# Attention ahead of two MoE layers: row sums' epsilon on ScalarE, separate tiles for maxima, a later start for GpSimd

## The chip, the cores and the metric

The kernel runs on one core of one Trainium2 chip. The metric is the device time of one execution in microseconds; less is better. Engines are named as the profile names them: PE (TensorE matmuls), PEld (TensorE weight loads), DVE (VectorE), ACT (ScalarE), POOL (GpSimd), SP (SyncE, which issues the DMAs).

## The reference

Block-causal attention with 4 batches, 8 heads, 576 positions and a head dimension of 64, then two MoE-like layers on the 2304 tokens of 512 features. All is float32.

```python
scores = scale * np.matmul(q, k.transpose(0, 1, 3, 2))
scores = np.where(block_i >= block_j, scores, -1000000000.0)   # blocks of 64
scores = scores - np.max(scores, axis=-1, keepdims=True)
attn = np.exp(scores)
attn = attn / (np.sum(attn, axis=-1, keepdims=True) + 1e-09)
out = np.matmul(attn, v)
...
h = x @ w_in;  x = (h * np.clip(h + 3.0, 0.0, 6.0) / 6.0) @ w_out
h = x @ w_in2; x = (h * np.tanh(np.log1p(np.exp(h)))) @ w_out2
```

## The kernel before, in words

**Numbers as two parts.** Matmul operands are split into a high part and a remainder in the matmul's type (`hi = copy(x)`, `lo = x - hi`); a product is three matmuls, hi x hi, hi x lo and lo x hi. So each operand costs a copy on ACT or POOL and a subtraction on DVE or POOL.

**Attention.** Two heads that share 128 partitions are a pair; there are 16 pairs (`NP`), and five rounds to each, so 80 rounds g (`NG`). A round handles one or two query blocks of 64 (`PARTS`, in the order `TIME`): a big part and, in four of five rounds, a small one; together 320 or 640 columns of scores.

- `scores(g)` (L431) makes the scores in one of two PSUM tiles `s` (L442 to L444, three matmuls each). Then for each part DVE takes the negated maximum into a column of `nm` (L454), and ACT takes the exp with this maximum as bias, writes `p` and leaves the row sum in a column of `su` (L463). An exp is followed by an instruction that reads the accumulator.
- `transposes(g)` (L472) transposes `p` on PE (L495) into one of three PSUM banks `t`, from where ACT copies the high part to `z` (L281) and DVE subtracts the remainder (L287).
- `attn_v` (L505) multiplies with V into the PSUM tile `o` (L526), four calls for each pair; ACT copies `o` to `x` (L281), and DMAs store it.
- `sums(p)` (L539) takes the nine row sums of a pair (128 x 9), adds 1e-9 on DVE (L546), takes the reciprocal on DVE (L547), transposes on PE (L548) into a `t` bank, and ACT copies the result to `rs`.
- `split_q`, `split_k` and `split_v` prepare a pair's inputs. For pair 0 ACT and DVE split the queries (L372, L375) and ACT the high part of the keys (L397); the keys' remainder goes to DVE or POOL (L404). For later pairs all of it is POOL's work, and the split queries reach `qb` by two DMAs from `qs` (L388).
- `early_weights` (L559) prepares two of the first MoE layer's weight tiles in four pieces, in the rounds named by `EARLY_ROUNDS`.

**What sets the order.** The loop at L611 adds the operations of each round to a list: transposes of round g - `LAG_T` ahead of the scores when `FIRST_T` is true, behind them when it is not; the sums of a pair at a lag of `LAG_R` rounds; attention times V at a lag of `LAG_V`. `Schedule.order` (L129) then plans all engines with a table of costs (L64) and latencies. An operation's due time follows from the TensorE work listed ahead of what needs it; each engine takes, among the operations that are ready, the one due first. PE may choose among its next 40 (`AHEAD`) listed operations until the first MoE layer's second product begins, and goes by the list from there on. The planned order is then issued: each engine works through its own queue in this fixed order. The semaphores between engines are put in afterwards, from the tiles that the instructions read and write; one tile is one thing to wait for.

**MoE layers.** Behind attention the same list continues with the first MoE layer (`in1`, `out1`), whose weights are loaded and split while it runs, with the preparation of the second layer's weights beside it (`unit2`), and then the second layer (`in2`, `out2`). Their tiles take the memory of the attention tiles once these are closed (hooks `leave_scores` and `leave_attention`).

Of the kernel before, what the change touches and what calls it, by code (L numbers as in the profile page):

```python
# [9 lines left out]
F32 = mybir.dt.float32  # L10
F32R = mybir.dt.float32r
U32 = mybir.dt.uint32
AF = mybir.ActivationFunctionType
ALU = mybir.AluOpType
AX = mybir.AxisListType
# [3 lines left out]
P = 128  # L19
B, H, S, D = 4, 8, 576, 64  # L20
NB = S // 64
# [8 lines left out]
SCALE = 1.0 / math.sqrt(D)  # L30
# [15 lines left out]


LAND = 4500
EARLY_ROUNDS = (20, 32, 44, 56)
LAG_T, LAG_V, LAG_R, FIRST_T = 4, 10, 7, True  # L50

ALIGN = 96
NX = 384
# [161 lines left out]
def f32(ap):  # L215
    return ap.bitcast(F32)
# [7 lines left out]
def fused_kernel(ctx: ExitStack, tc: tile.TileContext, qT, kT, vv, w1, w2, outT):  # L224
    nc = tc.nc
# [13 lines left out]
    ident = cpool.tile([P, P], F32, tag="ident", name="ident")  # L239
# [25 lines left out]
    plan = Schedule()  # L265
# [19 lines left out]
    def sub(engines, reads, writes, dst, a, b, **kw):  # L285
        return plan.add(
            engines, reads, writes, lambda e: ENG[e].tensor_sub(*real(dst, a, b)), **kw)  # L287

    def matmuls(n, reads, writes, run):
        return plan.add((("PE", n, False),), reads, writes, run)  # L290
# [28 lines left out]
    for n in range(3):  # L319
        at["t", n] = ps_t.tile([P, 4, P], F32, tag="t", name=f"t{n}")  # L320
    for n in range(4):
        at["nm", n] = sm.tile([P, 2], F32, tag="nm", name=f"nm{n}")
    pairs = [(b, hp) for b in range(B) for hp in range(NPAIR)]
    NP = len(pairs)
    EARLY_TILES = (
# [34 lines left out]
    def warm():  # L360
        for n in range(20):
            nc.tensor.transpose(at["t", 0][:, n % 4, :], ident, ident)

    def split_q(p):
        n = p % 2
        q, qs = at["q", n], at["qs"]
        if p == 0:
            for j in range(2):
                r = slice(64 * j, 64 * j + 64)
                src = q[r].rearrange("p (n d) -> p n d", d=64)  # L370
                hi, lo = at["qb", 0][r, 0, :, r], at["qb", 0][r, 1, :, r]
                copy(S, [("q", n), ("qb", 0, j)], [("qb", 0, j, 0)], hi, src, scale=SCALE)  # L372
                plan.add(
                    one("DVE", "DVE", S), [("q", n), ("qb", 0, j, 0)], [("qb", 0, j)],
                    lambda e, lo=lo, src=src, hi=hi: nc.vector.scalar_tensor_tensor(  # L375
                        lo, src, SCALE, f32(hi), op0=ALU.mult, op1=ALU.subtract))
            return
        plan.add(
            one("POOL", "POOL_ONE", S), [("q", n)], [("q", n)],
            lambda e: nc.gpsimd.tensor_scalar(q, q, SCALE, 1.0, op0=ALU.mult, op1=ALU.mult))  # L380
        plan.add(
            one("POOL", "POOL_ONE", S), [("q", n)], [("qs", 0)], lambda e: nc.gpsimd.tensor_scalar(
                qs[:, 0, :], q, 1.0, 1.0, op0=ALU.mult, op1=ALU.mult))
        sub(one("POOL", "POOL", S), [("q", n), ("qs", 0)], [("qs", 1)], qs[:, 1, :], q,
            f32(qs[:, 0, :]))
        for j in range(2):
            r = slice(64 * j, 64 * j + 64)
            dma(288, [("qs", 0), ("qs", 1)], [("qb", n, j)], f32(at["qb", n][r, :, :, r]),  # L388
                f32(qs[r]).rearrange("p t (n d) -> p t n d", d=64), land=LAND)

    def split_k(p):
        n = p % 2
        k, kb = at["k", n], at["kb", n]

        def first(e):
            if e == "ACT":
                nc.scalar.activation(kb[:, 0, :], k, AF.Copy)  # L397
            else:
                nc.gpsimd.tensor_scalar(kb[:, 0, :], k, 1.0, 1.0, op0=ALU.mult, op1=ALU.mult)

        plan.add(
            one("ACT", "ACT", S) if p == 0 else one("POOL", "POOL_ONE", S), [("k", n)],
            [("kb", n, 0)], first)
        sub(either(S) if p == 0 else one("POOL", "POOL", S), [("k", n), ("kb", n, 0)],  # L404
            [("kb", n, 1)], kb[:, 1, :], k, f32(kb[:, 0, :]))

    def split_v(p):
        n = p % 2
        for i in range(2):
            r, c = ((slice(0, P), slice(0, 4)), (slice(0, 64), slice(4, 5)))[i]  # L410
            src = at["v", n][r, c, :].rearrange("p c (h d) -> p (c h) d", h=2)
            dst = at["vb", n][r, c].rearrange("p c h t d -> p (c h) t d")
            hi, lo = dst[:, :, 0, :], dst[:, :, 1, :]
            w = (512, 128)[i]
            plan.add(
                one("POOL", "POOL_V", w), [("v", n, i)], [("vb", n, i, 0)],
                lambda e, hi=hi, src=src: nc.gpsimd.tensor_scalar(
                    hi, src, 1.0, 1.0, op0=ALU.mult, op1=ALU.mult))
            sub(one("POOL", "POOL", w), [("v", n, i), ("vb", n, i, 0)], [("vb", n, i, 1)],
                lo, src, f32(hi))  # L420

# [9 lines left out]
    def scores(g):  # L431
# [5 lines left out]
        for i, _, o, banks in score_parts(m):  # L437
            n = 64 * (i + 1)
            for a, z, b in ((o, 512, 0), (512, o + n, 1)) if len(banks) == 2 else ((o, o + n, banks[0]),):
# [4 lines left out]
                    nc.tensor.matmul(sc[:, cs], ql[:, i, :], kb[:, 0, ks], start=False, stop=True)  # L444

                matmuls(3 * cost("S", z - a), names, [("s", g % 2)], run)
        nm, su = at["nm", g % 4], at["su", p % 2]
        t, w = parts[m]
        todo = score_parts(m)
        for i, c, o, banks in todo:  # L450
            n = 64 * (i + 1)
            plan.add(
                one("DVE", "DVE_PSUM", n), [("s", g % 2)], [("nm", g % 4, c)],
                lambda e, o=o, n=n, c=c: nc.vector.tensor_reduce(  # L454
                    nm[:, c:c + 1], sc[:, o:o + n], axis=AX.X, op=ALU.max, negate=True))
        for i, c, o, banks in todo:
            n = 64 * (i + 1)
            col = ORDER.index(i)
            dst = t[:, w:w + n] if c else t[:, 0:n]
            plan.add(  # L460
                one("ACT", "EXP", n), [("s", g % 2)] + [("nm", g % 4, c), ("pz", m, c)],
                [("p", m, c), ("su", p % 2, col)],
                lambda e, o=o, n=n, c=c, col=col, dst=dst: nc.scalar.activation(  # L463
                    dst, sc[:, o:o + n], AF.Exp, bias=nm[:, c:c + 1], accum_out=su[:, col:col + 1]))

    bank = [0]

# [71 lines left out]
    def sums(p):  # L539
        b, hp = pairs[p]  # L540
        su, rs, k = at["su", p % 2], at["rs", p % 2], next_bank()
        tp = at["t", k]
        cols = [("su", p % 2, i) for i in range(NB)]
        plan.add(
            one("DVE", "DVE", NB), cols, cols,
            lambda e: nc.vector.tensor_scalar(su, su, 1e-9, None, op0=ALU.add))  # L546
        plan.add(one("DVE", "DVE", NB), cols, cols, lambda e: nc.vector.reciprocal(su, su))  # L547
        matmuls(cost("T", P), cols, [("t", k)], lambda e: nc.tensor.transpose(tp[0:NB, 0, :], su, ident))  # L548
        copy(P, [("t", k)], [("rs", p % 2)], rs, tp[0:NB, 0, :], psum=True)
        dma(4, [("rs", p % 2)], [("rsd", hp, b)],  # L550
            rsd[hp, :, b * S:(b + 1) * S].rearrange("h (n q) -> n h q", q=64),
            rs.rearrange("n (h q) -> n h q", h=2))

    def prepare(p):
        if p < NP:
            split_k(p)
            split_q(p)

# [656 lines left out]
```

## Time and profile before

| | |
|---|---|
| median of 3 runs | 964.37 us (964.29 to 970.2) |
| profiled execution: its time / its span | 966.9 / 965.0 us |
| busy over the span | PE 940.8 (97%), PEld 855.0 (89%), DVE 619.7 (64%), ACT 535.1 (55%), POOL 610.4 (63%) |
| DMA | 212.88 MB, 221 GB/s in the mean |
| attention, about | 9 to 215 us |

The span runs from the first to the last instruction of the profiled execution; its time includes what lies around it. An engine's busy time counts its instructions, not its waits. In the view in order of time each row has the start and the length in us, the engine, the line, the operation, the tiles written and read, the shape, the number of instructions that were merged, and in brackets the idle time of the engine just before and what ended it. A row of POOL is rough in its length. Line 281 is the helper that makes every ACT copy and line 287 the one that makes the subtractions, so those rows are told apart by their tiles.

### The profile page before, as it was taken

To read this page: it belongs to the slowest core of one execution; us is meant where nothing else is said; L and a number is where in the kernel's file an instruction comes from. 1 tells how busy PE (TensorE), PEld (TensorE's weight loads), DVE (VectorE), ACT (ScalarE), POOL (GpSimd) and SP (SyncE) were. 2 spreads that over 40 slices of the span, in tenths; PEclk is the share of its full clock that TensorE was granted. 3 is DMA by queue.
4 is the path that set the end of the run, shared out by engine and by line. 5 is a ranking of instruction groups with operands and counts; after the bars stand their busy time and mean duration, and the time that the engine had idled before them with its cause. 6 is when DMAs were issued, how large, how long until landed. Compare 5 with 4: busy or idle time off the path is not lost.

```text
span 965.0 us, 15989 instructions
## 1 busy us (share of the span) xinstructions
PE 940.8 (97%) x5300; PEld 855.0 (89%) x5300; DVE 619.7 (64%) x1150; ACT 535.1 (55%) x1254; POOL 610.4 (63%) x640
## 2 busy tenths in 40 slices
PE   7989999999999999999999999999999999999998
PEld 6878888888888887877788899999999999999997
DVE  6778777778875566556422235566578756876567
ACT  5878888886765455454332243544464444644452
POOL 8577777636888556844500013386798876967875
PEclk9999999999999999999999999999999999999999
DMA  9597897459648898888610016776778876787752
GB/s 244 146 248 204 189 233 200 116 163 366 251 151 260 290 302 287 287 300 282 192 50 1 0 45 234 262 265 225 266 261 306 311 265 234 262 306 261 262 200 95
DMA packets 131426, 212.88 MB, mean 221 GB/s; under 512 B 45840, under 2 KB 72464, under 8 KB 131344
## 3 DMA queue, kind: packets, MB, share of 16 engines
q1 hardware_dynamic: 131344, 211.86, 68.1%
q8 instruction: 42, 0.69, 0.3%
q14 instruction: 40, 0.33, 0.1%
HBM read 154.66 MB, written 48.31 MB: 210 GB/s over the span
## 4 chain that ended last, share of the span: by engine, by line
PE 49%; DVE 1%; DMA 1%; ACT 0%; issue 0%; POOL 0%; DVEq 0%; POOLq 0%; SPq 0%
PE y L687 8%; PE y L688 8%; PE y L689 8%; PE h L687 5%; PE h L688 5%; PE h L689 5%; PE r L689 3%; PE r L688 3%; PE r L687 3%; DMA S<-x2d 1%; DVE o L1027 0%; POOL S L287 0%; DMA w2d<-S 0%; DVE e L287 0%; ACT X L281 0%
## 5 line engine op out<-in xcount | busy, mean ns | idle before, releaser
L687 PE MATMUL h<-X,wh 128*128 128x512 f32 (+1 forms) x320 | 119.6, 374 | 0.8 <-DVE gl L287 0.5
L688 PE MATMUL h<-X,wh 128*128 128x512 f32 (+1 forms) x320 | 118.0, 369 | 0.3 <-POOL X L287 0.3
L689 PE MATMUL h<-X,wl 128*128 128x512 f32 (+1 forms) x320 | 118.0, 369 | 0.0
L688 PE MATMUL y<-gl,wh 128*128 128x512 f32 (+1 forms) x320 | 117.7, 368 | 0.0
L687 PE MATMUL y<-gh,wh 128*128 128x512 f32 (+1 forms) x320 | 117.7, 368 | 0.0
L689 PE MATMUL y<-gh,wl 128*128 128x512 f32 (+1 forms) x320 | 117.7, 368 | 0.0
L687 PE MATMUL y<-X,wh 128*128 128x384 f32 x336 | 112.5, 335 | 1.1 <-ACT xs L281 0.9
L688 PE MATMUL y<-X,wh 128*128 128x384 f32 x336 | 112.5, 335 | 0.0
L689 PE MATMUL y<-X,wl 128*128 128x384 f32 x336 | 112.3, 334 | 0.0
L287 POOL TENSOR_TENSOR X<-xr,X 128x384 fp32r<-128x384 f32 (+2 forms) x35 | 38.0, 1088 | 110.9 <-ACT X L281 110.9
L793 DVE SCALAR_TENSOR_TENSOR h<-e,h 128x512 f32<-128x512 f32 (+1 forms) x64 | 40.1, 627 | 89.9 <-ACT e L281 89.8
L463 ACT ACTIVATE p<-s,nm 128x576 f32<-128x576 f32 (+2 forms) x144 | 76.0, 529 | 31.7 <-DVE nm L454 29.9
L1027 DVE TENSOR_TENSOR sgh<-y,sgh 128x384 f32<-128x384 f32 x129 | 69.6, 555 | 33.2 <-PE y L689 33.2
L287 DVE TENSOR_TENSOR z<-t,z 128x512 fp32r<-128x512 f32 (+3 forms) x144 | 73.0, 521 | 19.9 <-ACT z L281 18.5
L454 DVE TENSOR_REDUCE nm<-s 128x1 f32<-128x576 f32 (+2 forms) x144 | 67.1, 480 | 26.2 <-PE s L444 13.0
L281 ACT ACTIVATE e<-h 128x512 f32<-128x512 f32 (+1 forms) x80 | 43.9, 549 | 66.5 <-PE h L689 66.5
L287 POOL TENSOR_TENSOR X<-e,X 128x384 fp32r<-128x384 f32 x69 | 71.3, 1034 | 10.9 <-ACT X L281 10.9
L495 PE MATMUL t<-ident,p 128*128 128x128 f32 x400 | 66.6, 283 | 7.6 <-DVE z L287 6.6
L687 PEld LDWEIGHTS h<-X,wh 128*128 128x128 f32 x320 | 60.3, 189 | 14.3 <-DVE gl L287 4.8
L689 PEld LDWEIGHTS h<-X,wl 128*128 128x128 f32 x320 | 60.4, 189 | 10.4 <-DVE wl L740 0.2
L688 PEld LDWEIGHTS h<-X,wh 128*128 128x128 f32 x320 | 60.4, 189 | 10.2 <-POOL X L287 0.7
L689 PEld LDWEIGHTS y<-gh,wl 128*128 128x128 f32 x320 | 60.3, 188 | 10.0
(166 smaller groups left out, 2679.2 us busy)
## 6 DMA issues: line engine op xcount, KB each, us to landing
raw<-w SPq DMA_DIRECT2D x64, 512.0 KB
wh<-w2d SPq DMA_DIRECT2D x48, 512.0 KB
wl<-w2d SPq DMA_DIRECT2D x48, 512.0 KB
wh<-w2d SPq DMA_DIRECT2D x48, 384.0 KB
wl<-w2d SPq DMA_DIRECT2D x48, 384.0 KB
x1d<-x SPq DMA_DIRECT2D x64, 144.0 KB
qb<-qs SPq DMA_DIRECT2D x30, 288.0 KB
w2d<-Sh SPq DMA_DIRECT2D x32, 256.0 KB
```

The lines of the kernel that those rows point to most:

```text
L281: nc.scalar.activation(d, s, func, **kw)
L287: engines, reads, writes, lambda e: ENG[e].tensor_sub(*real(dst, a, b)), **kw)
L454: lambda e, o=o, n=n, c=c: nc.vector.tensor_reduce(nm[:, c:c + 1], sc[:, o:o + n], axis=AX.X, op=ALU.max, negate=True))
L463: lambda e, o=o, n=n, c=c, col=col, dst=dst: nc.scalar.activation(dst, sc[:, o:o + n], AF.Exp, bias=nm[:, c:c + 1], accum_out=su[:, col:co ...
L495: nc.tensor.transpose(tp[:, c, :], t[:, o:o + P], ident)
L687: nc.tensor.matmul(b, wh, xh, start=start and k == 0, stop=False, skip_group_check=True)
L688: nc.tensor.matmul(b, wh, xl, start=False, stop=False, skip_group_check=True)
L689: nc.tensor.matmul(b, wl, xh, start=False, stop=last, skip_group_check=True)
L793: nc.vector.scalar_tensor_tensor(g, e, 6.0, h, op0=ALU.min, op1=ALU.mult)
L1027: nc.vector.tensor_add(dst, src, old)
```

## The change

The maxima of the two parts of a round get a tile each, `nm0` and `nm1` (four buffers each), instead of two columns of one. In `sums`, ACT copies the nine sums with 1e-9 added into a `t` bank in PSUM, DVE takes the reciprocal from there back into `su`, and the transposition goes to another column group of the same bank. At the start, POOL's splits of the queries and keys of pair 1 and of the values of pairs 0 and 1 wait until the keys of pair 0 are split, and the remainder of these keys is DVE's alone. Pair 0's queries are listed ahead of its keys. The rounds of the early weights and the lags change: transposes of g - 3 are listed behind the scores of g, where transposes of g - 4 were listed ahead of them, and attention times V follows at 8 rounds instead of 10.

```diff
--- before.py
+++ after.py
@@ -46,8 +46,8 @@
 
 
 LAND = 4500
-EARLY_ROUNDS = (20, 32, 44, 56)
-LAG_T, LAG_V, LAG_R, FIRST_T = 4, 10, 7, True
+EARLY_ROUNDS = (25, 35, 45, 55)
+LAG_T, LAG_V, LAG_R, FIRST_T = 3, 8, 7, False
 
 ALIGN = 96
 NX = 384
@@ -319,7 +319,8 @@
     for n in range(3):
         at["t", n] = ps_t.tile([P, 4, P], F32, tag="t", name=f"t{n}")
     for n in range(4):
-        at["nm", n] = sm.tile([P, 2], F32, tag="nm", name=f"nm{n}")
+        for c in range(2):
+            at["nm", n, c] = sm.tile([P, 1], F32, tag=f"nm{c}", name=f"nm{c}_{n}")
     pairs = [(b, hp) for b in range(B) for hp in range(NPAIR)]
     NP = len(pairs)
     EARLY_TILES = (
@@ -361,8 +362,11 @@
         for n in range(20):
             nc.tensor.transpose(at["t", 0][:, n % 4, :], ident, ident)
 
+    start = []
+
     def split_q(p):
         n = p % 2
+        first = start if p == 1 else ()
         q, qs = at["q", n], at["qs"]
         if p == 0:
             for j in range(2):
@@ -377,7 +381,8 @@
             return
         plan.add(
             one("POOL", "POOL_ONE", S), [("q", n)], [("q", n)],
-            lambda e: nc.gpsimd.tensor_scalar(q, q, SCALE, 1.0, op0=ALU.mult, op1=ALU.mult))
+            lambda e: nc.gpsimd.tensor_scalar(q, q, SCALE, 1.0, op0=ALU.mult, op1=ALU.mult),
+            after=first)
         plan.add(
             one("POOL", "POOL_ONE", S), [("q", n)], [("qs", 0)], lambda e: nc.gpsimd.tensor_scalar(
                 qs[:, 0, :], q, 1.0, 1.0, op0=ALU.mult, op1=ALU.mult))
@@ -400,9 +405,11 @@
 
         plan.add(
             one("ACT", "ACT", S) if p == 0 else one("POOL", "POOL_ONE", S), [("k", n)],
-            [("kb", n, 0)], first)
-        sub(either(S) if p == 0 else one("POOL", "POOL", S), [("k", n), ("kb", n, 0)],
+            [("kb", n, 0)], first, after=start if p == 1 else ())
+        last = sub(one("DVE", "DVE", S) if p == 0 else one("POOL", "POOL", S), [("k", n), ("kb", n, 0)],
             [("kb", n, 1)], kb[:, 1, :], k, f32(kb[:, 0, :]))
+        if p == 0:
+            start.append(last)
 
     def split_v(p):
         n = p % 2
@@ -415,7 +422,7 @@
             plan.add(
                 one("POOL", "POOL_V", w), [("v", n, i)], [("vb", n, i, 0)],
                 lambda e, hi=hi, src=src: nc.gpsimd.tensor_scalar(
-                    hi, src, 1.0, 1.0, op0=ALU.mult, op1=ALU.mult))
+                    hi, src, 1.0, 1.0, op0=ALU.mult, op1=ALU.mult), after=start if p < 2 else ())
             sub(one("POOL", "POOL", w), [("v", n, i), ("vb", n, i, 0)], [("vb", n, i, 1)],
                 lo, src, f32(hi))
 
@@ -444,7 +451,7 @@
                     nc.tensor.matmul(sc[:, cs], ql[:, i, :], kb[:, 0, ks], start=False, stop=True)
 
                 matmuls(3 * cost("S", z - a), names, [("s", g % 2)], run)
-        nm, su = at["nm", g % 4], at["su", p % 2]
+        su = at["su", p % 2]
         t, w = parts[m]
         todo = score_parts(m)
         for i, c, o, banks in todo:
@@ -452,7 +459,7 @@
             plan.add(
                 one("DVE", "DVE_PSUM", n), [("s", g % 2)], [("nm", g % 4, c)],
                 lambda e, o=o, n=n, c=c: nc.vector.tensor_reduce(
-                    nm[:, c:c + 1], sc[:, o:o + n], axis=AX.X, op=ALU.max, negate=True))
+                    at["nm", g % 4, c], sc[:, o:o + n], axis=AX.X, op=ALU.max, negate=True))
         for i, c, o, banks in todo:
             n = 64 * (i + 1)
             col = ORDER.index(i)
@@ -461,7 +468,7 @@
                 one("ACT", "EXP", n), [("s", g % 2)] + [("nm", g % 4, c), ("pz", m, c)],
                 [("p", m, c), ("su", p % 2, col)],
                 lambda e, o=o, n=n, c=c, col=col, dst=dst: nc.scalar.activation(
-                    dst, sc[:, o:o + n], AF.Exp, bias=nm[:, c:c + 1], accum_out=su[:, col:col + 1]))
+                    dst, sc[:, o:o + n], AF.Exp, bias=at["nm", g % 4, c], accum_out=su[:, col:col + 1]))
 
     bank = [0]
 
@@ -541,18 +548,21 @@
         su, rs, k = at["su", p % 2], at["rs", p % 2], next_bank()
         tp = at["t", k]
         cols = [("su", p % 2, i) for i in range(NB)]
-        plan.add(
-            one("DVE", "DVE", NB), cols, cols,
-            lambda e: nc.vector.tensor_scalar(su, su, 1e-9, None, op0=ALU.add))
-        plan.add(one("DVE", "DVE", NB), cols, cols, lambda e: nc.vector.reciprocal(su, su))
-        matmuls(cost("T", P), cols, [("t", k)], lambda e: nc.tensor.transpose(tp[0:NB, 0, :], su, ident))
-        copy(P, [("t", k)], [("rs", p % 2)], rs, tp[0:NB, 0, :], psum=True)
+        nine = tp[:, 0, 0:NB]
+        copy(NB, cols, [("t", k)], nine, su, bias=1e-9)
+        plan.add(
+            one("DVE", "DVE_PSUM", NB), [("t", k)], cols, lambda e: nc.vector.reciprocal(su, nine))
+        matmuls(cost("T", P), cols, [("t", k)], lambda e: nc.tensor.transpose(tp[0:NB, 1, :], su, ident))
+        copy(P, [("t", k)], [("rs", p % 2)], rs, tp[0:NB, 1, :], psum=True)
         dma(4, [("rs", p % 2)], [("rsd", hp, b)],
             rsd[hp, :, b * S:(b + 1) * S].rearrange("h (n q) -> n h q", q=64),
             rs.rearrange("n (h q) -> n h q", h=2))
 
     def prepare(p):
-        if p < NP:
+        if p == 0:
+            split_q(p)
+            split_k(p)
+        elif p < NP:
             split_k(p)
             split_q(p)
 
```

## Rows read from the trace of the kernel before

**Rows 1.** Windows: length; busy us (count) of PE, PEld, DVE, ACT, POOL; clock; DMA.

```profile
50.00:200.00 150.00, 140.49 (x1028) 127.32 (x1027) 116.44 (x252) 126.08 (x400) 106.51 (x123) 1.00 0.77 193
...
225.00:965.00 740.00, 733.94 (x3874) 670.56 (x3872) 450.23 (x794) 356.25 (x707) 455.92 (x457) 1.00 0.66 228
```

**Rows 2.** PE in order of time: first score matmul of six pairs.

```profile
18.98 0.27 PE L442 MATMUL s<-kb,qb 128*128 128x64 f32 x1 [0.28 <-ACT p L463]
...
29.96 0.27 PE L442 MATMUL s<-kb,qb 128*128 128x64 f32 x1
...
40.34 0.28 PE L442 MATMUL s<-kb,qb 128*128 128x64 f32 x1
...
51.61 0.28 PE L442 MATMUL s<-kb,qb 128*128 128x64 f32 x1
...
91.75 0.27 PE L442 MATMUL s<-kb,qb 128*128 128x64 f32 x1 [0.41 <-POOL vh L287]
...
187.93 0.27 PE L442 MATMUL s<-kb,qb 128*128 128x64 f32 x1
```

**Rows 3.** Waits, 9 to 200 us: us in total, times, longest.

```profile
ACT p L463 <- DVE nm L454: 29.9, 50, 5.2
...
DVE nm L454 <- ACT p L463: 12.6, 24, 0.8
```

**Rows 4.** Groups by line, 9 to 200 us: busy us, mean ns, idle before.

```profile
L546 DVE TENSOR_SCALAR su<-su 128x9 f32<-128x9 f32 x15 | 12.7, 849 | 0.0
...
L281 ACT ACTIVATE rs<-t 9x128 f32<-9x128 f32 x15 | 3.8, 250 | 0.0
...
L281 ACT ACTIVATE t<-raw 128x512 f32<-128x512 f32 x4 | 2.5, 637 | 0.0
L281 ACT ACTIVATE wh<-val 128x512 fp32r<-128x512 f32 x4 | 2.5, 634 | 0.0
```

**Rows 5.** Tile `su`: duration in ns, least, median and most.

```profile
L546 DVE TENSOR_SCALAR su<-su x16: 159/566/2324, 24.0 to 203.4; 128x9 f32<-128x9 f32 x16
L547 DVE RECIPROCAL su<-su x16: 197/216/218, 24.9 to 203.7; 128x9 f32<-128x9 f32 x16
```

**Rows 6.** In order of time: around the addition of 82.73, then two late exps.

```profile
80.84 0.75 DVE L454 TENSOR_REDUCE nm<-s 128x1 f32<-128x576 f32 x1
...
82.73 2.32 DVE L546 TENSOR_SCALAR su<-su 128x9 f32<-128x9 f32 x1
...
84.34 0.68 POOL L382 TENSOR_SCALAR qs<-q 128x576 fp32r<-128x576 f32 x1
...
86.14 0.69 ACT L463 ACTIVATE p<-s,nm 128x512 f32<-128x512 f32 x1 [1.60 <-DVE nm L454]
...
60.35 0.69 ACT L463 ACTIVATE p<-s,nm 128x512 f32<-128x512 f32 x1 [1.88 <-DVE nm L454]
...
182.47 0.69 ACT L463 ACTIVATE p<-s,nm 128x512 f32<-128x512 f32 x1 [0.89 <-DVE nm L454]
```

**Rows 7.** DVE and ACT in order of time: a maximum and its exp.

```profile
97.97 1.09 DVE L454 TENSOR_REDUCE nm<-s 128x1 f32<-128x128 f32 x3 [0.44 <-ACT p L463]
...
98.29 0.37 ACT L463 ACTIVATE p<-s,nm 128x128 f32<-128x128 f32 x1 [0.36 <-DVE nm L454]
```

**Rows 8.** All engines in order of time, the start.

```profile
4.17 0.68 POOL L380 TENSOR_SCALAR q<-q 128x576 f32<-128x576 f32 x1
...
5.06 3.02 DVE L375 SCALAR_TENSOR_TENSOR qb<-q,qb 64x576 fp32r<-64x576 f32 x2 [1.21 <-ACT qb L281]
...
6.66 0.68 ACT L397 ACTIVATE kb<-k 128x576 fp32r<-128x576 f32 x1 [0.93 <-DMA k<-kT]
...
8.12 1.10 DVE L287 TENSOR_TENSOR kb<-k,kb 128x576 fp32r<-128x576 f32 x1
...
9.27 0.42 PE L443 MATMUL s<-kb,qb 128*128 128x64 f32 x1 [1.44 <-DVE kb L287]
...
15.64 0.67 POOL L382 TENSOR_SCALAR qs<-q 128x576 fp32r<-128x576 f32 x1 [1.32 <-DMA qb<-qs]
```

## The prediction

> **What bounds the kernel now.** I read the stretches first, then the starts of the pairs, then the waits, then single instructions. From 225 us to the end TensorE is busy 733.94 of 740 us [rows 1]: the two MoE stages are bound by TensorE, and the change touches nothing in them. In the attention stage (50 to 200 us) TensorE is busy 140.49 of 150, ScalarE 126.08 and VectorE 116.44 [rows 1]. TensorE's matmuls overlap and their ends are modelled, so some of its slack is hidden in that 140.49; the stage is a ring in which the two score tiles pass from TensorE to VectorE (maximum), to ScalarE (exp), and back.
>
> The ring's pace is the distance between the first score matmuls of two pairs. Pair 1 starts at 18.98 and pair 15 at 187.93, 168.95 us for 14 pairs, 12.07 each; the quickest pair takes 10.38 (29.96 to 40.34) [rows 2]. Pairs 1 to 3 take 10.88 each (18.98 to 51.61), pairs 4 to 6 13.38 (51.61 to 91.75), the last eight 12.02 (91.75 to 187.93) [rows 2]. What is late in the ring is seen in the waits from 9 to 200 us: ScalarE's exp waited for a maximum 29.9 us in 50 waits (the longest, 5.2, is the start), and a maximum waited for an exp 12.6 us in 24 waits [rows 3]. The second looks backward: a maximum needs only its scores.
>
> **Row sums.** Line 546 adds the epsilon on VectorE: nine numbers per partition, 159 ns when undisturbed, yet median 566 and at most 2324 ns; the reciprocal on the same tile takes 197 to 218 ns in all 16 cases [rows 5]. Fifteen additions hold VectorE 12.7 us [rows 4], 12.7 - 15 x 0.16 = 10.3 us more than undisturbed. The longest began at 82.73 and ended at 85.05, just after GpSimd's instruction of 84.34 had ended (85.02) [rows 6]. Behind it in VectorE's queue stood the reciprocal and the next maximum, and ScalarE's exp came 1.60 us late [rows 6]. Six of the 16 additions do this; the first such exp is 1.88 us late at 60.35, the last 0.89 at 182.47 [rows 6]; the six make 8.4 us of idle ScalarE. Three of them lie in pairs 4 to 6 and three in the last eight: the pairs that are 13.38 and 12.02 long instead of 10.88. Part of that excess is early weights and token work, so I do not take all of it.
>
> The change takes this addition off VectorE. Ends: 0 (TensorE works from another item while ScalarE idles) and 8.4 us (all of it is on the ring). I take 6.5, nearer to the upper end, because the long pairs are just those with the stalls: 3 x (13.38 - 10.88) = 7.5 us in pairs 4 to 6 alone. **-6.5.**
>
> The Trainium skill, "SBUF — State Buffer", Who interferes with whom, says that VectorE and GpSimd share a port pair as a lock, that a SBUF tensor_scalar can need it, and that the one that starts first holds it for one whole instruction. The trace agrees on who blocks, but not on how long: the 2.32 us row outlasts a whole GpSimd instruction and ends with the one of 84.34. By the rule alone each addition would wait for one instruction and the term would be under half; by the rows it is the 10.3 us above.
>
> **What the new sum step costs.** Added: 16 ScalarE copies of nine elements into PSUM. The trace has no such copy; below is nothing (ScalarE has 150 - 126.08 = 24 us idle in the stage), above is the copy of 128 elements out of PSUM, 250 ns [rows 4], so 16 x 0.25 = 4.0 us. A copy of 512 into PSUM takes 637 ns and one into SBUF 634 [rows 4], so the target does not matter. The reciprocal stays at about 0.22, now behind a ScalarE instruction: while it waits, the next maximum stands behind it. The transposition bank is held longer, from the ScalarE copy on rather than from the transposition. I take **+1.5**, near the middle, since ScalarE is the second busiest engine of the ring.
>
> The Trainium skill, "ScalarE: Activation LUTs", Step-by-step: what each stage is for, calls PSUM the lower-latency target for ScalarE. The rows (637 against 634 ns) show no difference; by the page this term would be a little smaller.
>
> **Maxima in tiles of their own.** Both columns of a negated maximum were one tile, and the order between engines is kept per tile. At 97.97 the maximum of 128 columns starts after 0.44 us of waiting for the exp of the other part, which only reads the other column, and its own exp at 98.29 is 0.36 us late [rows 7]. With two tiles this wait goes. 24 such waits cost VectorE 12.6 us [rows 3]; ScalarE's share is at most 24 x 0.36 = 8.6. Yet the quickest pair, 10.38, has the same shared tile, so most of this is hidden behind TensorE's own work. Ends 0 and 8.6, and I take **-2.0**. What is late next is the maximum's place behind the z subtractions in VectorE's queue.
>
> **Start.** VectorE's two query remainders take 3.02 us from 5.06, with GpSimd at work since 4.17; the key remainder runs 8.12 to 9.22, and at 9.27 the second score matmul starts [rows 8]. A VectorE instruction of 576 columns takes 0.75 when it reads PSUM [rows 6], so with GpSimd idle 2 x 0.75 for the queries (done at about 6.6) and 0.75 for the keys. The keys' high part is there at 6.66 + 0.68 = 7.34 [rows 8], so 7.42 + 0.75 = 8.17 instead of 9.22. **-1.0** (ends -1.1 and 0).
>
> Against it, GpSimd's first split of pair 1 moves from 4.17 to about 8.2, 4.0 us. Its query halves go through DMA: GpSimd's next write of that buffer was let go at 15.64 by this DMA [rows 8], so pair 1's queries were in place near 15.6, and would be near 19.6 now. Pair 1's scores began at 18.98 and want to begin at 18.0. Behind the same GpSimd queue stand pair 1's keys and the values of pairs 0 and 1, and SyncE issues the query DMAs in order, so its loads wait with them. Ends 0 (GpSimd is quicker when VectorE leaves it alone, and the keys may go after the queries) and 1.6; I take **+0.7**, the middle rounded down.
>
> **Order.** Transposing g-4 ahead of round g's scores and transposing g-3 behind them give the same sequence of the two; what differs is that attention times V stands two rounds earlier, before more slack is used up, and that early weights come in rounds 25 to 55 instead of 20 to 56, the same four pieces. Sums stay at lag 7, and split_q of pair 0 ahead of split_k follows the landing order. Ends -2 and +2 (one round of 10.88 / 5); I take **0**.
>
> **Sum.** -6.5 + 1.5 - 2.0 - 1.0 + 0.7 = -7.3 us. The profiled execution took 966.9 us around a span of 965.0, so it would take 959.6. The median of the runs is 964.37, 2.5 under the profiled one; 964.4 - 7.3 = 957.1. The time after attention should move up whole: the MoE stages' weights are loaded into memory that attention frees, so their chain starts earlier too. A measurement of this kernel can tell about 1%, 9.6 us, from no change.
>
> **Rivals.** *The ring comes free altogether.* All four stretches of [rows 2] get the pace of pairs 1 to 3: 168.95 - 14 x 10.88 = 16.6 us, less about 3.6 for the early weights and token work that pairs 1 to 3 do not have: 964.4 - 13 = 951.4. For it: the stalls sit in just the long pairs. Against: those pairs hold extra work, and ScalarE at 84% gets 16 copies more.
>
> *Hidden.* TensorE's 94% is the real bound of the stage, and ScalarE's idle time costs little: about a quarter of the -9.5 gains, 964.4 - 2 = 962.4. For it: 140.49 of 150. Against: the spread of 10.38 to 13.4 among pairs with equal score work.
>
> *The new hand-over is worse than the stall.* ScalarE's copy must first get a bank that VectorE's z subtraction frees, VectorE's reciprocal waits for ScalarE, and the next maximum stands behind it, once a pair. ScalarE may have an exp (0.69 in [rows 6]) and a copy (0.64 in [rows 4]) ahead, about 1.5 us with its accumulator read: 16 x 1.5 = 24 us of waiting VectorE for 12.7 removed. At half a microsecond of time each, as taken above, and with no other gain, +5.6: 970.0. It decides from 12.7 / 16 = 0.8 us of waiting per reciprocal. Against it: the planner puts the reciprocal where it expects the copy to be done, and ScalarE's in-order wait for its own accumulator needs no other engine.
>
> **How the numbers follow.** Forecast (4 to 10 us gained) 0.60; ring free 0.20; hidden 0.13; worse hand-over 0.07. The forecast's own range is 954.4 to 960.4. To hold the time 8 times in 10 the range takes in the ring set free on one side and the hidden case on the other: 951 to 964. Faster by over 1% (under 954.7): the ring free and the forecast's edge, 0.28. Slower by over 1% (over 974.0): a hand-over worse than priced, 0.05. Within 1%: 0.67.
>
> **What would show it.** Right: no VectorE tensor_scalar on the sums; reciprocals near 0.2 us with waits for ScalarE under 0.8; the maximum's waits for exp near 0 instead of 12.6; exp's waits for maxima under 20 instead of 29.9; pairs 4 to 6 near 11.5 each; second score matmul near 8.2; the stretch after attention as long as before. Wrong: pair 1's first score later than 18.98 because of the query DMA, an exp still over 1 us late after a reciprocal, long pairs although the addition is gone, or a stall in a MoE stage that takes the gain back.

## The result, and the profile after

The kernel after takes 954.15 us in the median (952.47 to 956.55) beside 965.4 for the kernel before: a ratio of 0.9876 (of the means; the medians give 0.9883), interval 0.9833 to 0.9919. Its profiled execution took 952.47 us around a span of 949.9, 1.7 under that median, while the one of before lay 1.5 above 965.4; so the two spans differ by 15.1 us where the medians differ by 11.2.

The first line of the page, and the windows that answer to [rows 1] (the second ends at 945, since the span is shorter):

```profile
PE 935.0 (98%) x5300; PEld 857.0 (90%) x5300; DVE 610.1 (64%) x1133; ACT 534.8 (56%) x1270; POOL 609.5 (64%) x641
```

```profile
50.00:200.00 150.00, 147.17 (x1085) 135.79 (x1085) 115.87 (x255) 133.52 (x438) 116.83 (x132) 1.00 0.83 214
...
225.00:945.00 720.00, 718.94 (x3822) 661.95 (x3821) 439.57 (x774) 351.32 (x695) 441.60 (x444) 1.00 0.65 223
```

TensorE is now busy 147.17 of the 150 us of the attention stage (140.49 before): it is the bound there too. The starts of pairs that answer to [rows 2], PE in order of time:

```profile
18.93 0.27 PE L449 MATMUL s<-kb,qb 128*128 128x64 f32 x1 [0.24 <-ACT p L470]
...
51.32 0.27 PE L449 MATMUL s<-kb,qb 128*128 128x64 f32 x1
...
85.62 0.27 PE L449 MATMUL s<-kb,qb 128*128 128x64 f32 x1 [0.26 <-ACT p L470]
...
178.12 0.27 PE L449 MATMUL s<-kb,qb 128*128 128x64 f32 x1
```

Pair 15 starts at 178.12 instead of 187.93; 14 pairs take 159.19 us, 11.37 each for 12.07. Pairs 4 to 6 (51.32 to 85.62) take 11.43 each where they took 13.38. The first three take as long as before (10.80 for 10.88): the pairs have become alike, not quick.

Waits from 9 to 200 us, beside [rows 3]:

```profile
DVE z L287 <- ACT z L281: 35.7, 61, 1.1
...
ACT p L470 <- DVE nm L461: 10.6, 14, 5.0
...
DVE nm L461 <- ACT p L470: 1.7, 6, 0.3
```

The exp's waits for maxima fell from 29.9 to 10.6 us, of which 5.0 is the start; the maxima's waits for an exp from 12.6 to 1.7. The longest is now the remainder of `z` on DVE, which waits for ACT's copy; DVE has the time. The tile `su`, beside [rows 5] (least, median and most in ns):

```profile
L281 ACT ACTIVATE t<-su x16: 170/173/224, 24.1 to 193.9; 128x9 f32<-128x9 f32 x16
L554 DVE RECIPROCAL su<-t x16: 209/220/222, 24.3 to 194.4; 128x9 f32<-128x9 f32 x16
```

In place of 16 additions of up to 2324 ns stand 16 copies of 173, and no reciprocal is shown waiting.

**Where the 15.1 us arose.** The same work of TensorE can be followed in both kernels: the last score matmul, then the 65th of the matmuls `h<-X,wh` of the first MoE layer, then the last of these. The first fence is the kernel before, the second the kernel after:

```profile
199.03 0.31 PE L444 MATMUL s<-kb,qb 128*128 128x320 f32 x1
...
248.86 0.39 PE L687 MATMUL h<-X,wh 128*128 128x512 f32 x1
...
604.68 0.28 PE L688 MATMUL h<-X,wh 128*128 128x256 f32 x1
```

```profile
188.51 0.31 PE L451 MATMUL s<-kb,qb 128*128 128x320 f32 x1
...
238.33 0.39 PE L697 MATMUL h<-X,wh 128*128 128x512 f32 x1
...
590.00 0.28 PE L698 MATMUL h<-X,wh 128*128 128x256 f32 x1
```

Attention ends 10.5 us earlier. The passage, from the end of the last score to the 65th `h<-X,wh`, is as long as before (49.5 us). Then the first MoE layer gains 4.2 us more (355.82 to 351.67). From 320 to 610 us the waits of the kernel before have

```profile
PEld h L687 <- DVE gl L287: 4.8, 11, 0.9
```

and those of the kernel after have no such row: the remainder of the activated `h` came late from VectorE, which is busy 84.70 us from 350 to 500 in the kernel before and 80.22 in the kernel after. This second gain is not an accident of one trace. The stretch from the 191st `h<-X,wh` to the last takes 268.0 us in the kernel after, 268.0 to 269.2 in the five kernels below that keep its new lags and its sums in PSUM, and 270.2 to 272.7 in before and the seven others.

### The profile page after: what moved, and what is told of

Same layout as the page of the kernel before. It is cut to its first block, busy times and chain, and to the rows that moved or that the text cites. A ratio compares the mean times of both kernels' runs of the same rounds, so it can differ in the third digit from the quotient of the medians.

```text
span 949.9 us, 16054 instructions
## 1 busy us (share of the span) xinstructions
PE 935.0 (98%) x5300; PEld 857.0 (90%) x5300; DVE 610.1 (64%) x1133; ACT 534.8 (56%) x1270; POOL 609.5 (64%) x641
## 4 chain that ended last, share of the span: by engine, by line
PE 87%; ACT 4%; DMA 4%; DVE 3%; issue 1%; POOL 1%; SPq 0%; DVEq 0%; POOLq 0%; ACTq 0%
PE y L697 13%; PE y L698 13%; PE y L699 13%; PE h L699 10%; PE h L698 10%; PE h L697 10%; PE o L533 4%; PE t L502 3%; PE r L699 3%; PE r L698 3%; PE r L697 3%; ACT p L470 2%; PE s L449 2%; PE s L451 2%; PE s L450 2%; DMA raw<-w 1%
## 5 line engine op out<-in xcount | busy, mean ns | idle before, releaser
L287 POOL TENSOR_TENSOR X<-xr,X 128x384 fp32r<-128x384 f32 (+2 forms) x36 | 40.0, 1113 | 106.7 <-ACT X L281 106.6
L287 DVE TENSOR_TENSOR z<-t,z 128x256 fp32r<-128x256 f32 (+3 forms) x144 | 71.7, 525 | 36.0 <-ACT z L281 35.7
L470 ACT ACTIVATE p<-s,nm 128x576 f32<-128x576 f32 (+2 forms) x144 | 75.3, 528 | 11.7 <-DVE nm L461 10.6
L287 POOL TENSOR_TENSOR X<-e,X 128x384 fp32r<-128x384 f32 x69 | 70.8, 1027 | 10.9 <-ACT X L281 10.9
L698 PEld LDWEIGHTS y<-gl,wh 128*128 128x128 f32 x320 | 60.3, 188 | 10.2 <-POOL gl L287 0.4
L697 PEld LDWEIGHTS y<-gh,wh 128*128 128x128 f32 x320 | 60.3, 189 | 10.0
```

The costliest lines, as they stand in the source:

```text
L697: nc.tensor.matmul(b, wh, xh, start=start and k == 0, stop=False, skip_group_check=True)
L698: nc.tensor.matmul(b, wh, xl, start=False, stop=False, skip_group_check=True)
```

## The experiments

All were timed in turn with the kernel before, in three groups: a1 to a3 with e2, the b runs with d1, and c1, e1, f1 and g1. Times are best compared within a group. The kernel after itself is in none of them; e2 (953.18), b2 and d1 (953.17 and 953.78) and e1 (952.54), which differ from it by small edits, stand for it there. Line numbers differ by a few between the kernels.

**One part alone, put into the kernel before.**

*a1: the new sum step* (the copy into PSUM, the reciprocal from it, the other column group).

```diff
-            one("DVE", "DVE", NB), cols, cols,
-            lambda e: nc.vector.tensor_scalar(su, su, 1e-9, None, op0=ALU.add))
...
+        copy(NB, cols, [("t", k)], nine, su, bias=1e-9)
...
+            one("DVE", "DVE_PSUM", NB), [("t", k)], cols, lambda e: nc.vector.reciprocal(su, nine))
```

> The kernel before with the new sum step alone. Theory 1 (the stalled additions set the pace of the long pairs): the long exps after a reciprocal are gone, pairs 4 to 6 fall from 13.38 to under 12.3, pair 15 starts 5 to 7 us earlier than 187.93, and the time falls 0.5 to 0.7%. Theory 2 (the new order of work does it, the stall was hidden): pair 15 within 2 us of 187.93 and the time within 0.2%. Theory 3 (the hand-over between ScalarE and VectorE costs what the stall cost): exp waits stay near 29.9 us.

Measured: 960.62 us, ratio 0.9954 (0.9939 to 0.9968), 4.4 us under the 965.04 of before in its group. Attention gains all that the whole change gains: the last score ends at 188.12. The exp's waits for maxima fall by 11.0 us, but the reciprocal now waits for ScalarE's copy:

```profile
ACT p L463 <- DVE nm L454: 18.9, 35, 5.9
...
DVE su L547 <- ACT t L281: 2.6, 8, 0.9
```

And the passage takes 55.1 us for 49.5. PE in order of time in it:

```profile
200.44 1.51 PE L526 MATMUL o<-z,vh 128*128 128x320 f32 x10 [0.47 <-ACT x L281]
...
208.92 0.39 PE L689 MATMUL h<-X,wl 128*128 128x512 f32 x1
210.44 0.50 PE L687 MATMUL y<-gh,wh 128*128 128x512 f32 x1 [1.14 <-ACT gh L281]
211.80 0.64 PE L688 MATMUL y<-gl,wh 128*128 128x512 f32 x1 [0.86 <-POOL gl L287]
212.24 0.63 PE L689 MATMUL y<-gh,wl 128*128 128x512 f32 x1
212.66 0.63 PE L687 MATMUL y<-gh,wh 128*128 128x512 f32 x1
```

TensorE reaches the first product `y` before its operands are there, and after the two idle times the matmuls follow each other at 0.43 us instead of 0.23. The windows of a1 (columns as in [rows 1]):

```profile
190.00:200.00 10.00, 8.81 (x55) 7.24 (x55) 4.34 (x10) 8.21 (x24) 9.48 (x10) 1.00 0.46 128
205.00:210.00 5.00, 4.27 (x18) 2.84 (x16) 1.93 (x3) 2.40 (x5) 1.29 (x2) 1.00 0.84 307
210.00:215.00 5.00, 3.70 (x9) 2.71 (x10) 4.04 (x7) 3.67 (x7) 3.46 (x3) 0.70 0.65 193
```

and of the kernel after:

```profile
190.00:200.00 10.00, 10.00 (x71) 8.94 (x70) 6.22 (x13) 7.51 (x24) 2.57 (x2) 1.00 0.54 155
205.00:210.00 5.00, 5.00 (x23) 3.83 (x22) 4.35 (x8) 3.22 (x7) 3.21 (x4) 1.00 0.55 163
210.00:215.00 5.00, 5.00 (x23) 3.91 (x21) 2.45 (x5) 2.71 (x5) 2.27 (x3) 1.00 0.90 304
```

In a1 GpSimd is busy 9.48 of the 10 us from 190 on with token work and weights, in the kernel after 2.57. The granted clock of 0.70 in 210 to 215 is a mean of the two levels, 3 us at 1.2 GHz. So the sum step removes 11 us from attention, and 5.6 of them come back behind it.

*a2: the maxima's tiles.*

```diff
-        at["nm", n] = sm.tile([P, 2], F32, tag="nm", name=f"nm{n}")
+        for c in range(2):
+            at["nm", n, c] = sm.tile([P, 1], F32, tag=f"nm{c}", name=f"nm{c}_{n}")
```

> The kernel before with the maxima in tiles of their own alone. Theory 1: the maximum's waits for exp fall from 12.6 to under 3 us, the long additions stay, pair 15 starts 1 to 3 us earlier, the time falls 0.1 to 0.3%. Theory 2: the same waits fall, pair 15 within 1 us of 187.93.

Measured: 965.05 us, 1.0007 (0.9997 to 1.0017). Its waits from 9 to 200 us still have

```profile
DVE nm L455 <- ACT p L464: 13.3, 25, 0.9
```

so two tiles alone do not even remove the wait for which I had priced them. The maximum of [rows 7] waits here as long as before, 0.44 us, though its tile is now its own; what it waits for is not known.

```profile
99.24 1.08 DVE L455 TENSOR_REDUCE nm<-s 128x1 f32<-128x128 f32 x3 [0.44 <-ACT p L464]
```

*a3: the lags and the rounds of the early weights.*

```diff
-EARLY_ROUNDS = (20, 32, 44, 56)
-LAG_T, LAG_V, LAG_R, FIRST_T = 4, 10, 7, True
+EARLY_ROUNDS = (25, 35, 45, 55)
+LAG_T, LAG_V, LAG_R, FIRST_T = 3, 8, 7, False
```

> The kernel before with the lags and the rounds of the early weights alone. Theory 1: the additions still stall, and pair 15 starts within 2 us of 187.93; the time within 0.2%. Theory 2 (attention times V two rounds earlier and evenly spaced early weights): pair 15 starts 6 to 10 us earlier and the time falls 0.6 to 1.1%.

Measured: 959.43 us, 0.9951 (0.9936 to 0.9966), as much as the sum step. The profiled execution is the slowest of all its runs, 964.94, so its trace shows more delay than the median has; in it pair 15 starts at 185.88, 2 us earlier than before, which neither theory had expected together with such a time. The additions on VectorE are still there, yet hold it only 7.8 us (12.9 before), and most pairs take about 11.6. One, pair 10, takes 16.1 (122.7 to 138.8): a product of the token work that the plan put on VectorE waits there for 3.00 us, and the next remainders of `z`, then TensorE, stand behind it. The view puts the wait down to a GpSimd tile that the product does not read; the load of its `xn` was issued only at 128.54, so a late input is the likely reason, not a shown one.

```profile
132.58 1.19 DVE L831 TENSOR_TENSOR xr<-xr,xn 128x512 f32<-128x512 f32 x1 [3.00 <-POOL qs L382]
...
128.54 1.26 SPq L274 DMA_DIRECT2D xn<-rsd  x1
```

**One part undone in the kernel after.**

*b1: the old sum step.* The diff of a1, reversed.

> The kernel after with the sum step of before. Theory 1 (the stalled additions set the pace of the attention stage, whatever the order): additions hold VectorE 8 us or more again, pair 15 starts 4 to 8 us later than 178.12, the time is 0.5% over the kernel after. Theory 2 (in the new order the additions meet GpSimd elsewhere and cost little, as in the run with the order alone, where they held VectorE 7.8 us): pair 15 within 3 us of 178.12, time within 0.3% of the kernel after.

Measured: 959.60 us, 0.9948 (0.9929 to 0.9967). The additions are back (median 578 ns, most 1191, 9.2 us in all), most pairs take 11.6, and pair 10 takes 16.9 (in a profiled execution of 962.92 us, 3.3 over the median). All engines in order of time in that pair:

```profile
133.31 1.52 DVE L841 TENSOR_TENSOR xr<-xr,xn 128x512 f32<-128x512 f32 x1 [2.94 <-POOL qs L387]
...
134.86 0.63 ACT L281 ACTIVATE X<-xr 128x512 fp32r<-128x512 f32 x1 [3.86 <-DVE xr L841]
...
135.21 1.12 PE L502 MATMUL t<-ident,p 128*128 128x128 f32 x4 [3.17 <-DVE z L287]
```

The wait of one VectorE instruction stops all three engines of the ring. In the kernel after the nearest such product, at 135.67, is GpSimd's, and the two that VectorE got from 9 to 205 us wait for nothing.

*b2: one tile for both maxima.* The diff of a2, reversed.

> The kernel after with both maxima in one tile. Theory 1 (the waits of maxima for exps are hidden, as the tiles alone moved nothing): the waits come back (1.7 to 5 us or more), pair 15 within 1 us of 178.12, time within 0.2% of the kernel after. Theory 2 (once the stalls are gone these waits are next): pair 15 starts 2 us and more later, time 0.2% and more over the kernel after.

Measured: 953.17 us, 0.9868 (0.9848 to 0.9887), no slower than the kernel after, 0.9876. And with the shared tile the waits are

```profile
DVE nm L460 <- ACT p L469: 1.4, 5, 0.3
```

With a2 this is plain: the other parts moved the maxima, and the tiles did nothing.

*b3: the old lags and early rounds.* The diff of a3, reversed.

> The kernel after with the lags and early rounds of before. Theory 1 (the order's share lies in the passage to the MoE stage, not in the pairs): pair 15 within 2 us of 178.12, but the 65th matmul of the first MoE product, 49.5 us after the last score in the kernels before and after, comes 53 us or more after it, as with the sums alone (55.1); time 0.4% over the kernel after. Theory 2 (the order shortens the pairs): pair 15 starts 4 us and more later.

Measured: 961.76 us, 0.9962 (0.9948 to 0.9975). As in a1 attention is quick (last score 188.67) and the passage long, 56.2 us. PE in order of time shows the same two waits:

```profile
212.06 0.51 PE L697 MATMUL y<-gh,wh 128*128 128x512 f32 x1 [0.78 <-ACT gh L281]
...
213.42 0.50 PE L698 MATMUL y<-gl,wh 128*128 128x512 f32 x1 [0.85 <-POOL gl L287]
```

The last attention times V begins 16.0 us after the last score here (204.65), 10.9 in the kernel after (199.69).

*d1: only the old early rounds.*

```diff
-EARLY_ROUNDS = (25, 35, 45, 55)
+EARLY_ROUNDS = (20, 32, 44, 56)
```

> The kernel after with the early weights in rounds 20, 32, 44, 56 but the new lags. Theory 1 (the lags bring the passage, the rounds little): time within 0.2% of the kernel after, pair 15 within 1.5 us of 178.12, the passage near 49.5. Theory 2 (the even spacing of the weights does it): passage 52 us or more or pair 15 3 us later, time 0.3% over the kernel after.

Measured: 953.78 us, 0.9878 (0.9861 to 0.9895), passage 49.5. That is 0.6 us over b2 in the same group and 8.0 under b3: the early rounds are worth under a microsecond, and what b3 undoes is the lags. In the trace pair 15 starts at 181.15, the 3 us later that the second theory had asked for; but it starts at 180.16 in e2 too, which has the new rounds, so one trace does not settle where in attention such a delay comes from.

*e2: the old start* (no holding back, the keys' remainder free to go to either engine, the keys listed first).

```diff
-        if p == 0:
-            split_q(p)
-            split_k(p)
-        elif p < NP:
+        if p < NP:
...
-            lambda e: nc.gpsimd.tensor_scalar(q, q, SCALE, 1.0, op0=ALU.mult, op1=ALU.mult),
-            after=first)
+            lambda e: nc.gpsimd.tensor_scalar(q, q, SCALE, 1.0, op0=ALU.mult, op1=ALU.mult))
```

> The kernel after with the start of before (no holding back of GpSimd, pair 0's keys listed ahead of its queries, the keys' remainder on either engine). Theory 1 (the holding back is in the plan alone, there is no wait on the chip, and GpSimd starts at 4.17 either way): second score matmul at 9.27 and pair 1 at 18.9 as in the kernel after, the time within 0.2% of it. Theory 2 (the start is worth its 1 us): slower by 1 us and more than the kernel after.

Measured: 953.18 us, 0.9882 (0.9862 to 0.9902), where the kernel after has 0.9876: no worth of the start edit can be seen.

**What the start edit did.** The kernel after, all engines in order of time, beside [rows 8]:

```profile
4.17 0.67 POOL L384 TENSOR_SCALAR q<-q 128x576 f32<-128x576 f32 x1
...
5.03 1.17 DVE L287 TENSOR_TENSOR kb<-k,kb 128x576 fp32r<-128x576 f32 x1 [1.18 <-ACT kb L402]
...
6.63 2.58 DVE L379 SCALAR_TENSOR_TENSOR qb<-q,qb 64x576 fp32r<-64x576 f32 x2 [0.43 <-ACT qb L281]
...
9.26 0.42 PE L451 MATMUL s<-kb,qb 128*128 128x64 f32 x1 [1.48 <-DVE qb L379]
```

GpSimd was not held back at all: it starts on pair 1's queries at 4.17 as before. `after=` is a rule for the planner alone; no tile passes between the two engines, so no semaphore is set. What changed is the order of the loads: the keys of pair 0 now land first, so the second score matmul runs at 7.50, and the third waits for the queries. That is not the start edit's doing either, since e2, without it, has the same order:

```profile
9.26 0.42 PE L450 MATMUL s<-kb,qb 128*128 128x64 f32 x1 [1.20 <-DVE qb L379]
```

*e1: a hold-back that is real.* A GpSimd instruction of one element reads the keys' remainder, and the splits are planned behind it.

```diff
-            start.append(last)
+            start.append(plan.add(
+                one("POOL", "POOL_ONE", 1), [("kb", 0, 1)], [("gate",)],
+                lambda e: nc.gpsimd.tensor_scalar(
+                    at["gate"], f32(kb[:, 1, 0:1]), 1.0, 1.0, op0=ALU.mult, op1=ALU.mult)))
```

> The kernel after with the holding back made real: a small GpSimd instruction reads the remainder of pair 0's keys before GpSimd splits anything of pair 1. Theory 1: the keys' remainder and the two query remainders take about 0.75 us each, the third score matmul moves from 9.26 to about 8.2, pair 1 starts between 17.8 (head start kept) and 19.5 (queries of pair 1 late by their DMA), time within 0.2% of the kernel after. Theory 2 (GpSimd's delay of 2 us and more goes through to the pairs): pair 1 later than 20, time 0.2% over.

Measured: 952.54 us, 0.9868 (0.9854 to 0.9882). GpSimd's first split is at 6.09, the third score matmul at 8.56 instead of 9.26, pair 1 at 18.46 instead of 18.93: some half a microsecond, which the median can't show beside the kernel after.

*f1: the loads of pair 0 issued first* (in the kernel after pair 1's queries are loaded ahead of them).

```diff
-        dma(288, [], [("q", n)], at["q", n], qT[p], land=LAND if p else 2600)
-        dma(288, [], [("k", n)], at["k", n], kT[p], land=LAND if p else 2600)
+        if p == 0:
+            for t, src in ("q", qT), ("k", kT):
+                nc.sync.dma_start(at[t, n], src[p])
+                plan.add(one("SP", "SP", 288), [], [(t, n)], lambda e: None, land=2600)
+            return
...
```

> The kernel after with the loads of pair 0's queries and keys issued ahead of pair 1's (before and after, pair 1's queries are issued first). Theory 1 (the start hangs on the landing of pair 0's inputs): the third score matmul moves from 9.26 to 7.2 to 8.2, pair 1 and all behind it 1 to 2 us earlier, time 0.1 to 0.2% under the kernel after. Theory 2 (the time of pair 1 is set by its own queries' DMA): pair 1 at 18.9 or later, no gain.

Measured: 949.95 us, 0.9843 (0.983 to 0.9856), 2.6 us under e1 in its group: the best of all. The third score matmul starts at 7.83, pair 1 at 17.48. With pair 1's queries landing later, GpSimd starts on them only at 6.43, so this order of the loads holds it back as well, and the two effects are not told apart. How the gain passes through is open too: f1 is 1.3 us ahead of e1 at the last score, but level with it at the 65th `h<-X,wh` (237.17 and 237.22).

The window from 10 to 50 us seems to show another difference, a granted clock of 1.00 where the kernel after has 0.94. The single matmuls at its start do not bear it out: the first fence is f1, the second the kernel after, and in both two matmuls of 512 columns start 0.42 to 0.43 us apart, as they do at the lower level in a1.

```profile
10.00:50.00 40.00, 38.31 (x265) 34.02 (x264) 29.36 (x67) 33.16 (x114) 31.21 (x40) 1.00 0.82 218
...
10.72 0.63 PE L455 MATMUL s<-kb,qb 128*128 128x512 f32 x1
11.15 0.63 PE L456 MATMUL s<-kb,qb 128*128 128x512 f32 x1
```

```profile
12.15 0.63 PE L450 MATMUL s<-kb,qb 128*128 128x512 f32 x1
12.57 0.63 PE L451 MATMUL s<-kb,qb 128*128 128x512 f32 x1
```

**Two of the new parts, changed.**

*c1: the epsilon by ScalarE into SBUF.* The reciprocal reads a tile `se` there.

```diff
-        nine = tp[:, 0, 0:NB]
-        copy(NB, cols, [("t", k)], nine, su, bias=1e-9)
+        nine = at["se", p % 2]
+        copy(NB, cols, [("se", p % 2)], nine, su, bias=1e-9)
```

> The kernel after, but ScalarE writes the sums with the epsilon into a tile of SBUF and the reciprocal reads that tile. Theory 1 (the stall was that of VectorE's addition beside GpSimd; PSUM has no part): reciprocals stay near 0.2 us, pair 15 within 1 us of 178.12, time within 0.2% of the kernel after. Theory 2 (a small VectorE instruction that reads SBUF is what stalls): reciprocals of 0.5 us and more in the median, the long exps back, time 0.4% over the kernel after.

Measured: 959.33 us, 0.9937 (0.9924 to 0.9949). No instruction on the sums is held up:

```profile
L281 ACT ACTIVATE se<-su x16: 193/214/237, 20.1 to 199.7; 128x9 f32<-128x9 f32 x16
L555 DVE RECIPROCAL su<-se x16: 198/206/209, 21.5 to 200.2; 128x9 f32<-128x9 f32 x16
```

And yet it is 6.8 us slower than e1 in its group, half the gain lost, as in b1 and a3: pairs of 11.6, and pair 10 takes 15.1, with the token product on VectorE again. The profiled execution (959.15) lies at the median here, so pair 10 is no mark of a slow execution:

```profile
131.16 0.69 DVE L842 TENSOR_TENSOR xr<-xr,xn 128x512 f32<-128x512 f32 x1 [2.69 <-issue]
...
132.24 0.66 PE L503 MATMUL t<-ident,p 128*128 128x128 f32 x4 [2.10 <-DVE z L287]
```

So not the stall alone makes the difference between b1 and the kernel after: a changed tile gives the planner another order, and that order holds the accident of pair 10. The copy and the reciprocal themselves cost about the same either way: 214 and 206 ns here, 173 and 220 in the kernel after. Which property of the step (the bank, its cost in the plan, its lag) makes the order good was not separated.

*g1: the lag of attention times V back to 10, the rest new.*

```diff
-LAG_T, LAG_V, LAG_R, FIRST_T = 3, 8, 7, False
+LAG_T, LAG_V, LAG_R, FIRST_T = 3, 10, 7, False
```

> The kernel after with attention times V at 10 rounds instead of 8. Theory 1 (the two rounds of V that are left behind the last score keep memory taken, so the weight loads and the MoE stage start late): the last V matmul comes 15 us or more after the last score instead of 12.3, the passage takes 53 us or more instead of 49.5, time 0.4 to 0.9% over the kernel after, pair 15 within 1.5 us of 178.12. Theory 2 (the transposes' lag and place bring the passage): passage near 49.5, time within 0.2%.

Measured: 967.29 us, 1.0018 (1.0007 to 1.0029). With the transposes listed behind the scores, a lag of 10 lets the pair after next overwrite parts of `z` before a pair's fourth product has read them; so part of the attention is computed from another pair's numbers, and the waits between transposes and products are others too. Pairs take 12.3, and the passage is 50.0, against the theory that the lag of 10 makes it long. But with a late last score (198.86) this kernel did not put that theory to the test it needed. In the kernel before, too, attention times V ends late (its last group begins at 213.38, 14.0 us after the last score) with a passage of 49.5, so late products with V alone do not make the passage long.

## Why the prediction was right, and where it was not

The time, 954.15, lies in the range and 3 us under the forecast of 957.1; the 1.2% gained is in the case "faster by over 1%", to which I gave 0.28. It lies just outside the forecast's own range (954.4 to 960.4), toward the ring set free.

**Row sums, -6.5 and +1.5.** The net was about right: -4.4 us alone (a1), and 5.8 to 6.4 beside the new lags (b1 against d1 and b2). The way there was not. In attention the step is worth 11.2 us (last score 199.34 to 188.12), more than the 8.4 of idle ScalarE that I took as the upper end. The mechanism is borne out in that the exp's waits for maxima fell by 11.0 us there; but the planned order changed with the step, and how much of this is the stalls and how much the order is not shown. The +1.5 for the hand-over is not to be seen in the kernel after: 16 copies of 0.173 are 2.8 us of ScalarE, and no reciprocal is shown waiting. With the old lags it is there: the reciprocal waits 2.6 us in a1 and in b3, the longest 0.9. The rival *new hand-over worse*, which needed 0.8 us of waiting per reciprocal, fell by that. The Trainium skill, "SBUF — State Buffer", Who interferes with whom, says of ScalarE that it waits for nobody at its ports; the trace agrees: the same nine numbers written by ScalarE into SBUF took 193 to 237 ns in c1, where VectorE's addition took up to 2324.

**"The time after attention should move up whole."** This failed for the sum step alone: 5.6 of the 11.2 us came back in the passage (a1, and 6.6 in b3). The row to read would have been the work behind the last score: GpSimd's 9.48 of 10 us of token work and the first `gh` and `gl`, which have to wait for their own chain however early TensorE arrives. In the kernel after the expected "stretch after attention as long as before" was wrong to the other side: from the 65th `h<-X,wh` to the span's end it is 4.6 us shorter.

**Order, 0 (-2 to +2).** The term that was mis-sized: -5.6 alone (a3), -8.0 beside the new sums (b3 against d1). I had valued the listing of the transposes and the two rounds of V as a shift by a fifth of a pair. What they changed is the whole planned order: shorter stalls of the additions (7.8 us for 12.9), no passage of 55 us. The transposes and the scores keep their sequence, as I wrote; but one more round of transposes now stands ahead of each round's sums and product with V (this is what spoils g1), and the planner starts from another list. d1 shows that the early rounds have next to no share (0.6 us). That V's shorter lag lets token work and the last products end earlier fits the windows of 190 to 200; it is argued, since g1 could not show it and the kernel before has late products with V and a short passage.

**Maxima, -2.0.** Nothing (a2, b2). The step that failed: "With two tiles this wait goes." It stayed, at 13.3 us, with two tiles (a2) and went, to 1.4, with one (b2).

**Start, -1.0 and +0.7.** Nothing that can be seen, because the hold-back never happened: I took a rule of the planner for a wait on the chip. The second score matmul forecast near 8.2 ran at 7.50, but the third, for which the ring waits, at 9.26. e1, with the real hold-back, comes near the forecast (8.56), and pair 1 gains 0.5 where I had a net 0.3; the feared delay of pair 1's queries did not come.

**The rivals.** *Ring free altogether* asked for pairs of 10.88 less the extra work; they take 11.37, 9.8 of 16.6 us. *Hidden* was wrong: TensorE's busy share rose from 94 to 98% as the waits went. So the sum came out near partly by errors that made up for each other: 2.3 us forecast for the maxima and the start that did not come, 5.6 to 8.0 of the order that were not forecast.

Sums and lags alone give 4.4 + 5.6 = 10.0 us, in the group in which the kernel after with the old start (e2) gains 11.9: nearly a plain sum. Left open: which property of the planner's input decides about the accident of pair 10; why the passage is long in a1 and b3 alone; and why the first MoE layer gains its 4 us only in the kernels with both parts (argued: what is loaded and split earlier is out of VectorE's way there).

## What to carry to other kernels

Price a change of lags or of tiles under a planner as a new order, not as the shift of one instruction: run each part alone and undone, and look for single instructions that hold a whole ring. Follow a gain past its stage to the first work of the next stage that has a chain of its own. A dependency that exists only in the plan holds nothing back on the chip; the start time of the first instruction it names tells whether it is real.

## What the runs showed of the hardware

Short idle times of TensorE can cost twice. In a1 two waits of 1.14 and 0.86 us were followed by about 3 us at the lower of the clock's two levels (0.70 granted in the mean of 210 to 215 us), in which matmuls followed each other at 0.43 us for 0.23. The stall of pair 10 did the same: behind TensorE's wait of 3.17 us in b1 the granted clock was 0.50 (the lower level) until 142 us, so the pair lost more than the wait.

```profile
135.20:141.90 6.70, 6.50 (x29) 6.07 (x30) 5.37 (x11) 5.59 (x19) 4.95 (x7) 0.50 0.70 171
```

Not every idle time does: g1 has a wait of 1.15 us in nearly every pair, and e2 one of 1.35 us (at 173.37), with 1.00 granted from 20 to 200 us in the one and from 170 to 180 in the other.

A window's clock of 1.00 near the start of a trace is no proof of the upper level: f1's row says 1.00 from 10 to 50 us, and its matmuls of 512 columns still start 0.43 us apart at 10.72 and 11.15.

A ScalarE copy of nine numbers per partition took 173 ns into PSUM (the kernel after) and 214 into SBUF (c1) in the median, where copies of 512 had shown no difference [rows 4]. The Trainium skill, "ScalarE: Activation LUTs", Step-by-step: what each stage is for, calls PSUM the quicker target; at this size the rows agree.
